# Two banks for scores, one pool of four banks for the other products, and a new written order in a decay-attention kernel with a gated convolution

## The chip, the core and the metric

The kernel runs on one core of a Trainium2 chip. The metric is device time in microseconds (us) of one execution; lower is better. A core has a matrix engine (TensorE, PE in the profile, with its weight loads as PEld), a vector engine (VectorE, DVE), an engine for functions (ScalarE, ACT), GpSimd (POOL) and SyncE (SP). In this kernel SP and POOL mostly issue transfers. Products of PE go to PSUM, which has eight banks of 128 x 512 float32. Only ACT and DVE take results out of it here.

## The reference, cut to what matters

Four batches, eight heads, 768 steps, head size 48. A state of 48 x 48 complex numbers decays step by step, takes in the outer product of key and value, and is read with the query. The result goes through a causal convolution of five taps, a sigmoid gate and two projections of 384 x 384. Everything is float32 and the weights of convolution and projections arrive as 64-bit numbers.

```python
mag = np.sqrt(a_re * a_re + a_im * a_im)
scale = np.minimum(mag, 0.999) / (mag + 1e-06)
a_re_n, a_im_n = (a_re * scale, a_im * scale)
for t in range(S):
    new_re = ar * S_re - ai * S_im
    new_im = ar * S_im + ai * S_re
    kv = np.einsum('bhd,bhe->bhde', k[:, :, t], v[:, :, t])
    S_re, S_im = (new_re + kv, new_im)
    y[:, :, t] = np.einsum('bhd,bhde->bhe', q[:, :, t], S_re)
...
for k in range(K):
    gate_pre += conv_w[k][None, None, :] * xp[:, k:k + S, :]
gate = 1.0 / (1.0 + np.exp(-gate_pre))
return (gate * (x @ w_val) @ w_out).astype(np.float32)
```

## The kernel before, in words

The decay of all steps up to t is a running sum of logarithms and angles, so the recurrence becomes a masked product of scaled queries and keys plus a carried state. The work is cut into ten units: eight groups of four heads, of which the first and the last are cut once more into two units of two heads. A unit goes through these steps, each named by a letter:

- **X, R, A, S, E, B** prepare it on ACT and DVE: logarithms, angles, sums along time (with small products on PE, `off`, that add the sums of earlier rows), sine and cosine, exponentials, and the scaled keys `kx` and queries (which take the place of `trig`). Small x, r, a are the same for odd units.
- **T** transposes one quarter of a head: three products with the identity into a tile `pt` (`L417`), which ACT copies into `kq` (`L418`). A unit of four heads has 16 of them, one of two heads 8.
- **s, k, t, y** work on a chunk of 128 steps, six to a unit: scores of keys and queries into `sc_ps` (`L445`, `L446`); the mask, by which DVE takes them out into `sm` (`L452`); the state, summed in `S_ps` and copied by ACT into `S_sb` (`L484` to `L487`); and the output in `y_ps`, from `sm` and the previous chunk's `S_sb`, copied by ACT into `y_sb` (`L465` to `L469`).
- **D** moves `y_sb` to the channel-major `xT` (`L499`, issued by POOL), **C** is the convolution on DVE (`L508`, `L511`), **G** the sigmoid on ACT, **M** one half of a projection step: the products `pv` with the first weight matrix, which DVE multiplies by the gate (`L532`), and `po` with the second, which ACT copies out (`L563`). **O** issues the store of the result.
- **W** converts the weights on DVE and ACT. **L, V, N** issue loads of inputs, values and re-laid keys, on SP.

The order in which all these steps are issued is the string `ORDER`, 991 letters long. Each letter asks its stream for one step; a step that may not go yet is passed over. At the end every instruction is tied to the one before it on its engine, so each engine works in the written order: an instruction that waits holds up all that stand behind it on that engine.

What binds the steps besides is the number of buffers. Scores have one bank (`PSC`), so the scores of a chunk may be issued only when the mask of the chunk before stands ahead of them, and run only when DVE has taken those out. The transposed tiles `pt` have two banks of their own. The pool `ps_m` has three, for `off`, `pv` and `po` (and `ps_t` lends a bank for `po` in the last batch). `S_ps` and `y_ps` have one each.

Of the kernel before, what the change touches and what calls it, by code (L numbers as in the profile page):

```python
# [22 lines left out]
    "XLXXLXxxxXXxxLxXxXRxrWLLWRRWLLRWWRAWRWrAWLWrAWrWRSSEErWaBWWrXWXWrSSWWXaWBBLWaXNWWWXVLNEWEWXBWWWW"  # L23
    "XTWXRRTRTTTRVWTtTWTBLRRtBskBWLLWRsWSWAStBxWLkTWAWyTxAskWyxWWTNETyskTETTytTtWBLtDBxxskysBLLtXksBT"
    "kxtWWXytTTyskNDxTTNWyXTTWXWskXxTtsVkyWXTDTXrytskTTWXRskrrRtytNTrTTtrTrRarSaskytLSDsRWaEVykRRERsk"
    "ytSsyBALBksBSLkBTCxsCyktTCDtNTxyTxTLTATxyTDTCxTLCtACTTtxTCTtTNCCTsCCCCCECxCkCVCGMMMMMsMyMksxrrrM"
    "EByMrLOMkstytBksrrBLXrDyMXkBLNMySMasTTkyTTDatXSTLOaCTNCCEMCTMTMXTMTXCMTTXtVTMTtTTEsBLtXCBOkMsBLX"
    "RyMkMxyxsBkRtTTyRtMxNRAsxxRTTkyAxstxtOkTxTNOrsTAkLTRDryMRSyLrMrTTaMTDOTtTTtTTsraaSECCCCCkCCCCCCC"
    "GMMMMMMsyEVkrMMsMOrSBLksyMOBNMMMByLMSkXysBXTkTtTTtEMTTyskTTyTTXXMtLXTTtNTTtTTsEBMDtLLDXCCBMksByM"
    "LxxkMyBskCtTXTsyVksxXCCRxtCTMORTNkDRyxMLtyRAsTTMxOkxRALyxrMTTAMtTrrMTRraTTtTTRtOTDCCCCCaCCOVrTrs"  # L30
    "kaCCCCCSSrSSGMMMMMMEsyEMkMsykMNyBDBsNBBTTktTOTsktCTtTCsTTCNMOykMECyMMCMCMysMksEBBBktMyMyOVstBkTT"
    "sMktNysktTTDCNCtCtyMytCMOTTsktTDCTsCkytDskyMsMkyMOyMDsMCCtMCCCCksCCCCCCGkOMstCyMCCCCCMGytkMMMyMM"
    "MMDOMOMMMMOCCCCCCGMMMMMMOMMOMOM"
# [12 lines left out]
def kernel(  # L46
# [33 lines left out]
    LB, MAINB, TMPB, KB, PSC, SMB, SSB, ZB, XB, KNB, VB, YB = 6, 3, 2, 6, 1, 2, 3, 4, 2, 3, 2, 2  # L80
    WL = 6
    TRIGB, KXB = 2, 1

# [7 lines left out]
    ps_t = fast.enter_context(tc.tile_pool(name="ps_t", bufs=2, space=PSUM))  # L91
    ps_s = fast.enter_context(tc.tile_pool(name="ps_s", bufs=PSC, space=PSUM))
    ps_S = fast.enter_context(tc.tile_pool(name="ps_S", bufs=1, space=PSUM))
    ps_y = fast.enter_context(tc.tile_pool(name="ps_y", bufs=1, space=PSUM))
    ps_m = fast.enter_context(tc.tile_pool(name="ps_m", bufs=3, space=PSUM))
# [132 lines left out]
    for t in y_ps + sc_ps:  # L228
        nc.vector.memset(t, 0.0)

# [172 lines left out]
    def transpose(u):  # L403

        b, h0, g = units[u]
        tl = tiles[u]
        for h in range(g):
            while not free_head():
                yield "wait"
            heads[0] += 1  # L410
            t = qkp.tile([C2, 2, S], F32, name="kq")
            tj = t.rearrange("c s (f p j) -> c s f p j", f=2, j=JH)
            for f in range(2):
                for s, src in enumerate((tl["kx"], tl["qx"])):
                    pt = ps_t.tile([P, JH, P], F32, name="pt")
                    for j in range(JH):
                        nc.tensor.transpose(pt[:C2, j, :], src[:, j, f, h, :], ident)  # L417
                    nc.scalar.copy(tj[:, s, f], pt[:C2].rearrange("c j p -> c p j"))  # L418
# [6 lines left out]
    class Attend:  # L425


        def __init__(self, u):
            self.u = u
            self.b, self.h0, self.g = units[u]  # L430
            self.tl = tiles[u]
            self.S_ps = None
            self.sc, self.sm, self.S_sb, self.y = {}, {}, {}, {}
# [40 lines left out]
        def state(self, n):  # L474
            if n == NCH - 1:
                return
            if n == 0:
                self.S_ps = ps_S.tile([P, 512], F32, name="S_ps")
            kn, vt = self.tl["kn"][n // HN], self.tl["v"]
            for h in range(self.g):  # L480
                c0 = (n % HN * self.g + h) * C2
                at_h = dict(start=(n == 0 and h == 0), stop=(n == NCH - 2), skip_group_check=True)
                cols = slice(h * D, (h + 1) * D)
                nc.tensor.matmul(self.S_ps[:64, cols], kn[:, c0:c0 + 64], vt[:, h, n], **at_h)  # L484
                nc.tensor.matmul(self.S_ps[64:C2 + 1, cols], kn[:, c0 + 64:c0 + C2 + 1], vt[:, h, n], **at_h)
            self.S_sb[n] = small.tile([C2, self.g * D], F32, name="S_sb", bufs=SSB)
            nc.scalar.copy(self.S_sb[n], self.S_ps[:C2, :self.g * D])  # L487
# [33 lines left out]
    def project(b, xT, t0, n, z, pool, psum, outs=None, ahead=None):  # L521
# [12 lines left out]
        if ahead:  # L534
            pvs = [psum.tile([P, 512], F32, name="pv", tag="mm") for _ in range(NT)]
# [19 lines left out]
        for m in range(t0, t0 + n, P):  # L555
            po = ps_t.tile([P, 512], F32, name="po", tag="pt") if ahead else psum.tile([P, 512], F32, name="po", tag="mm")
# [168 lines left out]
    def stream_c():  # L725
        for e in corder:
# [97 lines left out]
    def advance(key):  # L824
        if key in "skty":
# [160 lines left out]
```

## Time and profile before

| | us |
|---|---|
| median of three runs | 365.17 (364.27 to 367.84) |
| the profiled execution, its own time | 367.19 |
| span of its instructions | 365.5 |
| PE busy | 283.7 (78%) |
| DVE busy | 259.9 (71%) |
| ACT busy | 248.9 (68%) |
| POOL busy | 59.0 (16%) |

The durations used below are from the profiled execution, whose own time is 2.0 us over the median. PE stands still until the first unit is prepared (its first transposition starts at 31.4 us), and its last product ends at about 355 us; what remains of the span is the end of the program. A busy share is a mean over stretches with different limits, so the profile is read by stretches. The clock that PE was granted is either full or half; the profile gives its mean over a stretch.

### The profile page before, as it was taken

The numbers are of one execution on the slowest core, as the hardware profiler recorded it, in microseconds if no ns is written. First come the engines' busy times: TensorE is split into PE (matmuls) and PEld (weight loads), VectorE is DVE, ScalarE is ACT, GpSimd is POOL, SyncE is SP. The second block draws the span as 40 slices with busy tenths as digits, with TensorE's granted clock in tenths as the row PEclk, the third lists the DMA queues.
The fourth block names the chain that finished last, engine by engine and source line by source line (L and its number), as shares of the span: only waits on it lengthen the run. The fifth ranks groups of instructions, "written<-read, shape, count | busy, mean of one in ns | idle before, by whom it ended". The sixth has DMA issues, their size and how long they took to land.

```text
span 365.5 us, 8088 instructions
## 1 busy us (share of the span) xinstructions
PE 283.7 (78%) x3234; PEld 201.4 (55%) x3234; DVE 259.9 (71%) x339; ACT 248.9 (68%) x454; POOL 59.0 (16%) x147
## 2 busy tenths in 40 slices
PE   0120688486978699999979879999998999959970
PEld 0110466364766556756767447778765866745540
DVE  3699996837597799969886986389698657292310
ACT  5689678589599676998888777767978533441210
POOL 3000001011012200340123003302400340410210
PEclk9999996969799899999999989999999999988996
DMA  7944559778379752886949206669720526210210
GB/s 191 345 111 127 143 142 258 183 198 163 93 147 260 193 118 81 214 243 150 315 131 231 51 23 215 165 191 200 198 75 3 163 77 142 82 56 2 82 48 24
DMA packets 87804, 53.31 MB, mean 146 GB/s; under 512 B 36432, under 2 KB 84816, under 8 KB 87760
## 3 DMA queue, kind: packets, MB, share of 16 engines
q1 hardware_dynamic: 83664, 43.28, 45.8%
q0 software_dynamic: 4096, 9.44, 8.4%
q8 instruction: 27, 0.44, 0.5%
q14 instruction: 17, 0.14, 0.1%
HBM read 33.83 MB, written 14.16 MB: 131 GB/s over the span
## 4 chain that ended last, share of the span: by engine, by line
PE 23%; DVE 10%; issue 7%; DMA 6%; ACT 3%; POOL 2%; SPq 0%; POOLq 0%; DVEq 0%
PE po L242 6%; DVE z L511 4%; PE pt L417 3%; PE pv L242 3%; PE sc_ps L445 3%; DMA kn<-kd 3%; PE y_ps L465 3%; DMA xT<-y_sb 3%; PE y_ps L468 2%; POOL xT L499 1%; DVE kx L369 1%; DMA kd<-kx 1%; PE S_ps L484 1%; DVE z L508 1%; DVE sm L452 1%
## 5 line engine op out<-in xcount | busy, mean ns | idle before, releaser
L499 POOL DMA_DIRECT2D xT<-y_sb x80 | 40.6, 513 | 171.3 <-ACT y_sb L469 134.8
L418 ACT COPY kq<-pt 96x384 f32<-96x384 f32 x128 | 56.1, 476 | 17.6 <-PE pt L417 15.8
L452 DVE TENSOR_TENSOR sm<-sc_ps,mask 128x512 f32<-128x512 f32 (+1 forms) x60 | 34.8, 580 | 31.4 <-PE sc_ps L446 29.8
L242 PE MATMUL po<-wo_sb,z 128*64 128x384 f32 x288 | 52.1, 499 | 4.7 <-DVE z L532 4.6
L511 DVE SCALAR_TENSOR_TENSOR z<-xT,cw_sb,z 128x768 f32<-128x768 f32 (+1 forms) x60 | 51.4, 857 | 2.1
L445 PE MATMUL sc_ps<-kq 96*64 96x128 f32 x384 | 46.7, 287 | 7.9 <-DVE sm L452 7.8
L242 PE MATMUL pv<-xT,wv_sb 128*64 128x384 f32 x288 | 51.7, 505 | 0.0
L446 PE MATMUL sc_ps<-kq 96*64 96x64 f32 x384 | 44.5, 230 | 0.0
L417 PE MATMUL pt<-ident,kx 128*96 128x128 f32 x192 | 38.3, 314 | 8.0 <-DVE kx L369 7.6
L417 PE MATMUL pt<-ident,trig 128*96 128x128 f32 x192 | 36.2, 303 | 10.5 <-ACT tmp L284 5.4
L445 PEld LDWEIGHTS sc_ps<-kq 96*64 96x64 f32 x384 | 33.7, 143 | 18.0 <-DVE sm L452 12.5
L465 PE MATMUL y_ps<-kq,S_sb 96*48 96x128 f32 x320 | 36.7, 287 | 7.3 <-ACT y_sb L469 7.1
L468 PE MATMUL y_ps<-sm,v_in 128*48 128x128 f32 x384 | 41.2, 280 | 1.5 <-DVE sm L452 1.5
L469 ACT COPY y_sb<-y_ps 112x256 f32<-112x256 f32 (+1 forms) x60 | 19.5, 325 | 30.3 <-PE y_ps L468 28.9
L446 PEld LDWEIGHTS sc_ps<-kq 96*64 96x64 f32 x384 | 39.2, 142 | 0.0
L102 ACT ACT_TABLE_LOAD x28 | 35.9, 1283 | 1.3 <-PEq L970 0.8
L242 PEld LDWEIGHTS po<-wo_sb,z 128*64 128x64 f32 x288 | 24.0, 138 | 21.6 <-DVE z L532 6.6
L484 PE MATMUL S_ps<-v_in,kn 128*64 128x48 f32 x320 | 30.4, 234 | 6.1 <-ACT S_sb L487 4.2
L242 PEld LDWEIGHTS pv<-xT,wv_sb 128*64 128x64 f32 x288 | 22.6, 142 | 21.3 <-issue 14.6
L484 PEld LDWEIGHTS S_ps<-v_in,kn 128*64 128x64 f32 x320 | 25.4, 147 | 11.8 <-ACT S_sb L487 4.9
L417 PEld LDWEIGHTS pt<-ident,trig 128*96 128x96 f32 x192 | 23.1, 139 | 15.2 <-ACT kq L418 5.8
L417 PEld LDWEIGHTS pt<-ident,kx 128*96 128x96 f32 x192 | 21.2, 139 | 16.7 <-DVE kx L369 7.9
(83 smaller groups left out, 487.9 us busy)
## 6 DMA issues: line engine op xcount, KB each, us to landing
kd<-kx SPq DMA_DIRECT2D x12, 576.0 KB, 4.6
out_dram<-ot POOLq DMA_DIRECT2D x24, 192.0 KB, 2.4
ar_in<-in_a_re_dram SPq DMA_DIRECT2D x12, 288.0 KB, 4.0
ai_in<-in_a_im_dram SPq DMA_DIRECT2D x12, 288.0 KB, 5.9
k_in<-in_k_dram SPq DMA_DIRECT2D x12, 288.0 KB, 4.8
q_in<-in_q_dram SPq DMA_DIRECT2D x12, 288.0 KB, 4.5
xT<-y_sb POOLq DMA_DIRECT2D x48, 72.0 KB, 3.2
kd<-kx SPq DMA_DIRECT2D x8, 288.0 KB, 3.1
```

Source lines behind the costliest of these rows:

```text
L102: nc.scalar.preload_act_table_set(name)
L242: nc.tensor.matmul(out[c:c + 64], lhsT[:, c:c + 64], rhs, **kw)
L417: nc.tensor.transpose(pt[:C2, j, :], src[:, j, f, h, :], ident)
L418: nc.scalar.copy(tj[:, s, f], pt[:C2].rearrange("c j p -> c p j"))
L445: nc.tensor.matmul(sc[lo:lo + half, h, :], k[:, :half], q, start=True, stop=True)
L446: nc.tensor.matmul(sc[hi:hi + half, h, half:], k[:, half:], q[:, half:], start=True, stop=True)
L452: nc.vector.tensor_tensor(out=two(sm), in0=two(sc[:, :g]), in1=mask[:, :, None, :].to_broadcast([C, 2, g // 2, C]), op=ALU.mult)
L465: nc.tensor.matmul(o, self.S_sb[n - 1][:, h * D:(h + 1) * D], self.part(1, h, n), start=True, stop=False)
L468: nc.tensor.matmul(o, vt[:, h, n], sm[:, h, :], start=(n == 0), stop=True)
L484: nc.tensor.matmul(self.S_ps[:64, cols], kn[:, c0:c0 + 64], vt[:, h, n], **at_h)
L499: XQ.dma_start(out=xTs[b][c0 % P:c0 % P + c2 - c0, c0 // P, EXT + hf * HS:EXT + (hf + 1) * HS], in_=self.y[hf][r0:r0 + c2 - c0, h // 2],)
L511: nc.vector.scalar_tensor_tensor(out=z, in0=xT[:, c, EXT + t0 - t:EXT + t0 - t + n], scalar=cw_sb[:, TAPS - 1 - t, c:c + 1], in1=z, op0=AL ...
```

## The change

Five things are edited.

1. The scores get two banks (`PSC` 2): chunks take turns, and the scores of a chunk wait for the mask of the chunk before the last.
2. The pool `ps_t` of two banks is gone. `pt` now comes from `ps_m`, which has four banks instead of three. The sum of the banks is eight as before.
3. The state's bank is one tile for the whole kernel, `S_all`, set to zero once at the start by DVE, instead of a new tile for each unit.
4. `ORDER` is another string with the same letters, each as often as before (128 T, 104 M, 90 C, 60 each of s, k, t, y, and so on). Each kind of instruction on PE, DVE and ACT therefore comes as often as before, apart from one load of a function table more on ACT, and on DVE two more settings of a bank to zero. On POOL one small tile `zero` is set.
5. A function `keep_busy` is added, a product with zeros under the letter `w`. The letter does not stand in the new `ORDER`, so no such product is issued.

The core of the diff:

```diff
-    "XLXXLXxxxXXxxLxXxXRxrWLLWRRWLLRWWRAWRWrAWLWrAWrWRSSEErWaBWWrXWXWrSSWWXaWBBLWaXNWWWXVLNEWEWXBWWWW"
...
+    "LLXLXxxXXVxXLxxXXxxXRxrWWWWWLRWWRrrLWLVWRARRALWrarWraARSSWWWaWWWWWrSSEWEBBBLBWXWXEENXLNWTTTWTTWT"
...
-    LB, MAINB, TMPB, KB, PSC, SMB, SSB, ZB, XB, KNB, VB, YB = 6, 3, 2, 6, 1, 2, 3, 4, 2, 3, 2, 2
+    LB, MAINB, TMPB, KB, PSC, SMB, SSB, ZB, XB, KNB, VB, YB = 6, 3, 2, 6, 2, 2, 3, 4, 2, 3, 2, 2
+    MMB = 4
+    KEEP = 128
...
-    ps_t = fast.enter_context(tc.tile_pool(name="ps_t", bufs=2, space=PSUM))
-    ps_s = fast.enter_context(tc.tile_pool(name="ps_s", bufs=PSC, space=PSUM))
+    ps_t = None
+    ps_s = fast.enter_context(tc.tile_pool(name="ps_s", bufs=1, space=PSUM))
-    ps_m = fast.enter_context(tc.tile_pool(name="ps_m", bufs=3, space=PSUM))
+    ps_m = fast.enter_context(tc.tile_pool(name="ps_m", bufs=MMB, space=PSUM))
...
+    S_all = ps_S.tile([P, 512], F32, name="S_ps")
+    zero = const.tile([P, 64], F32, name="zero")
+    nc.gpsimd.memset(zero, 0.0)
-    for t in y_ps + sc_ps:
+    for t in y_ps + sc_ps + [S_all]:
         nc.vector.memset(t, 0.0)
+    def keep_busy():
+        nc.tensor.matmul(
+            S_all[:64, 512 - KEEP:], zero, dmat.rearrange("p f q -> p (f q)")[:, :KEEP],
+            start=False, stop=True, skip_group_check=True,
+        )
+        return True
...
-                    pt = ps_t.tile([P, JH, P], F32, name="pt")
+                    pt = ps_m.tile([P, 512], F32, name="pt", tag="mm")[:, :JH * P].rearrange("c (j p) -> c j p", j=JH)
...
-            if n == 0:
-                self.S_ps = ps_S.tile([P, 512], F32, name="S_ps")
...
-            po = ps_t.tile([P, 512], F32, name="po", tag="pt") if ahead else psum.tile([P, 512], F32, name="po", tag="mm")
+            po = psum.tile([P, 512], F32, name="po", tag="mm")
...
+        if key == "w":
+            return keep_busy()
```

How the new string moves instructions shows best at two places. The first is ACT where the copies of the sixth unit (unit 5 of 0 to 9) begin; `kq<-pt` is such a copy, `y_sb` and `S_sb` are the copies of an output and of a state, `ot` of a projection. Before:

```order
L469 COPY y_sb<-y_ps_133 112x2x128
L269 ACTIVATE tmp<-main 128x1152
L487 COPY S_sb<-S_ps 96x192
L418 COPY kq<-pt 96x384 x2
L469 COPY y_sb<-y_ps_133 112x2x128
L487 COPY S_sb<-S_ps 96x192
L563 COPY ot<-po 128x384
L276 ACTIVATE tmp,over<-main 128x1152
L279 ACTIVATE tmp<-tmp,b_one 128x1152
L418 COPY kq<-pt 96x384 x2
```

And now, at the same unit:

```order
L576 COPY ot<-po 128x384
L481 COPY y_sb<-y_ps_130 112x2x128
L292 ACTIVATE tmp<-tmp,b_one 128x1152
L431 COPY kq<-pt 96x384 x3
L481 COPY y_sb<-y_ps_130 112x2x128
L497 COPY S_sb<-S_ps 96x192
L431 COPY kq<-pt 96x384 x13
```

The 16 copies of a unit came in pairs between other steps and now come almost in one run, and their transpositions with them on PE. Outputs, states and projections that stood among the copies stand ahead of them or behind.

The second place is PE near the end of the last unit, from the scores of its fourth chunk on. `sc_ps_134` is the one bank of scores before; `sc_ps_131` and `sc_ps_132` are the two of now. Each row with `L445` or `L446` (now `L457`, `L458`) is a product of scores, and a chunk of this unit has four. Before:

```order
L485 MATMUL S_ps<-v_in,kn 33x48
L445 MATMUL sc_ps_134<-kq 64x128
L446 MATMUL sc_ps_134<-kq 64x64
L445 MATMUL sc_ps_134<-kq 64x128
L446 MATMUL sc_ps_134<-kq 64x64
L445 MATMUL sc_ps_134<-kq 64x128
L446 MATMUL sc_ps_134<-kq 64x64
L445 MATMUL sc_ps_134<-kq 64x128
L446 MATMUL sc_ps_134<-kq 64x64
L484 MATMUL S_ps<-v_in,kn 64x48
```

Now, where the last chunk's scores stand:

```order
L494 MATMUL S_ps<-v_in,kn 64x48
L495 MATMUL S_ps<-v_in,kn 33x48
L255 MATMUL pv<-xT,wv_sb 64x384 x12
L457 MATMUL sc_ps_132<-kq 64x128
L458 MATMUL sc_ps_132<-kq 64x64
L457 MATMUL sc_ps_132<-kq 64x128
L458 MATMUL sc_ps_132<-kq 64x64
L494 MATMUL S_ps<-v_in,kn 64x48
```

Before, the scores of two chunks stood back to back on one bank, so that the second had to wait for the mask of the first. Now twelve products `pv` and the chunk before stand between a bank's scores and its next ones.

More of the change, by code (lines that the diff above doesn't have):

```diff
@@ L22 @@
 ORDER = (
-    "XLXXLXxxxXXxxLxXxXRxrWLLWRRWLLRWWRAWRWrAWLWrAWrWRSSEErWaBWWrXWXWrSSWWXaWBBLWaXNWWWXVLNEWEWXBWWWW"
[L24 to L33, printed above, removed]
+    "LLXLXxxXXVxXLxxXXxxXRxrWWWWWLRWWRrrLWLVWRARRALWrarWraARSSWWWaWWWWWrSSEWEBBBLBWXWXEENXLNWTTTWTTWT"
+    "XTXTBLsskBXBWkyLWtBTskNXXLtRRxRyWskWWsWxTTxTRykWtRTxWxWxTWWTyLsWkWRtWTxytskxrrDyAttWsksARNSyktSr"
+    "DVysWtrAErysWrkWDErBLatBskSatBLyLSkaNByXEWWXyNWTTtDTTTTTTLTWTTTTXTTTtEstBLXsVBktkyXWsBLkWyBskxtX"
+    "yDstykWskNXytxWCCCCCTTXTyTTDTTTTxCCTCTTTTVTCTsktCxskCCLCCtNyCxCskCRRCLGMRMMsxtMykMxMyDRAARRsxrrr"
+    "ktRSSMMAOMMstrEEOryMrMBLMMrSSBNyaMBLLLOaXMtkXMMaMyMEMDBTTTTTTTTTTTTXTTXTTstEBLMsNtBkykBLxsOMxsNt"
+    "yVksXBkXtCysxkXtXyMxMkyxTTTyttTOCTTTTTCTTCTCMDDCOTNxTCTCTCCCCLRCCRCskRstCxCCGMMMMMMRskRtVykLRxrr"
+    "rMMORsykAMSyrDMSAAEaOrskrtMrMsOaEBMtLBNykMSyMaMtSEBLLXyBNXMMTTMTTTTTTLTTTTTTTTsEtMXDBLsXBkkBLXLx"
+    "txXyskCtysBXMOtCXRRyDskRxkCNtTtTVTTTTTTsxxRAyLRxCkCMANxRxrrAyMMMMOyDtTVTTTTTrTTRSSssCCktCyskCras"
+    "kECtOyCCsEBkrBCCtCCyDBskCtykNCGMaMaMMyMtByMCCCMMOCCCtTDTTTTTTTMsksrtrCNCSMVMCSskMMykOMCMMEEBCOsB"
+    "NsBtNMykMMCykMDyMstBTTTTTOTTkTtstykMyDssMtykkMMOtMCCyCsCksCtCCCCCCCOykDCtCCMGCCMstyMMCGMMyMkyMMt"
+    "MDMOOMMMMMOCCCCCCGMMMMMMMMOOMMO"
 )
@@ L431, in __init__ @@
             self.tl = tiles[u]
-            self.S_ps = None
             self.sc, self.sm, self.S_sb, self.y = {}, {}, {}, {}
@@ L483, in state @@
                 cols = slice(h * D, (h + 1) * D)
-                nc.tensor.matmul(self.S_ps[:64, cols], kn[:, c0:c0 + 64], vt[:, h, n], **at_h)
-                nc.tensor.matmul(self.S_ps[64:C2 + 1, cols], kn[:, c0 + 64:c0 + C2 + 1], vt[:, h, n], **at_h)
+                nc.tensor.matmul(S_all[:64, cols], kn[:, c0:c0 + 64], vt[:, h, n], **at_h)
+                nc.tensor.matmul(S_all[64:C2 + 1, cols], kn[:, c0 + 64:c0 + C2 + 1], vt[:, h, n], **at_h)
             self.S_sb[n] = small.tile([C2, self.g * D], F32, name="S_sb", bufs=SSB)
-            nc.scalar.copy(self.S_sb[n], self.S_ps[:C2, :self.g * D])
+            nc.scalar.copy(self.S_sb[n], S_all[:C2, :self.g * D])
         def collect(self, hf):
@@ L534, in project @@
         if ahead:
-            pvs = [psum.tile([P, 512], F32, name="pv", tag="mm") for _ in range(NT)]
+            pvs = [
+                psum.tile([P, 512], F32, name="pv", tag="mm")
+                for i in range(NT)
+            ]
             for ci in range(NT):
@@ L733, in stream_c @@
                 zs[b, c] = moe.tile([P, S], F32, name="z", bufs=ZB)
+                done["z", b, c] = True
             yield from conv(xTs[b], t0, n, c, zs[b, c][:, t0:t0 + n])
@@ L752, in stream_m @@
             if i in early:
-                while not (has_x(b, 0, t0 + n) and done.get("W") and done.get(("T", NU - 1)) and (b, NT - 1) in zs):
+                while not (has_x(b, 0, t0 + n) and done.get("W") and done.get(("T", NU - 1)) and done.get(("z", b, NT - 1))):
                     yield "wait"
```

## The prediction

> **What bounds the kernel now.** I read the page first, for the busy tenths of its 40 slices (9.1 us each) and the granted clock.
>
> ```profile
> PE   0120688486978699999979879999998999959970
> ACT  5689678589599676998888777767978533441210
> PEclk9999996969799899999999989999999999988996
> ```
>
> PE is nearly full in the second half and not in the first; ACT is the other way round. So I looked for the point where one takes over from the other, and found it at the copies of unit 5's transpositions. The next two fences are the timeline of ACT there and the stretches to either side (stretch: length, then busy time and count of PE, PEld, DVE, ACT and POOL, the granted clock, DMA).
>
> ```profile
> 179.42 0.30 ACT L487 COPY S_sb<-S_ps 96x192 f32<-96x192 f32 x1
> 179.62 0.86 ACT L418 COPY kq<-pt 96x384 f32<-96x384 f32 x2
> ```
>
> ```profile
> 31.40:179.60 148.20, 117.39 (x1326) 84.91 (x1328) 121.78 (x140) 119.72 (x206) 18.62 (x44) 0.92 0.70 180
> 179.60:355.00 175.40, 163.20 (x1880) 113.89 (x1877) 116.20 (x160) 106.00 (x216) 36.48 (x80) 0.97 0.43 116
> ```
>
> The copy at 179.62 follows the instruction before it with no idle time: ACT was the late one. Up to there each of the three engines is busy for 117 to 122 of 148 us, and none is full: a chain through all three sets the pace. From there PE is busy for 163.2 of 175.4 us, ACT and DVE for 106 and 116. The end is thus the moment at which ACT comes to unit 5's copies, plus what PE has left by then, plus some 12 us in which PE still stands idle.
>
> **The change part by part.** I make the sum against this execution, in differences, and apply them to the median: the execution took 367.19 us, 1.7 more than its span of 365.5, and 2.0 more than the median of 365.17.
>
> *What PE has left at unit 5.* In the written order of the two kernels I counted what stands on each engine ahead of unit 5's first transposition. On PE it is now, beyond what stood there before, six products `po` (one step), the scores and the outputs of three chunks of four heads, and the state of one. The timeline of a full stretch gives their prices by the starts.
>
> ```profile
> 244.90 2.11 PE L242 MATMUL po<-wo_sb,z 128*64 128x384 f32 x12
> 246.84 0.42 PE L465 MATMUL y_ps<-kq,S_sb 96*48 96x128 f32 x4
> 247.72 0.27 PE L445 MATMUL sc_ps<-kq 96*64 96x128 f32 x1
> 248.39 0.27 PE L484 MATMUL S_ps<-v_in,kn 128*64 128x48 f32 x2
> 248.93 0.53 PE L417 MATMUL pt<-ident,kx 128*96 128x128 f32 x3
> ```
>
> So `po` is 1.94, an output 0.88, scores 0.67, a state 0.54, and the sum is 1.94 + 3 x 0.88 + 3 x 0.67 + 0.54 = 7.1 us that PE no longer has ahead of it when unit 5 begins. On ACT the same count gives three `y_sb`, two `ot`, one `S_sb` and one full-width activation more, and two table loads less.
>
> ```profile
> L102 ACT ACT_TABLE_LOAD x28 | 35.9, 1283 | 1.3 <-PEq L970 0.8
> L469 ACT COPY y_sb<-y_ps 112x256 f32<-112x256 f32 (+1 forms) x60 | 19.5, 325 | 30.3 <-PE y_ps L468 28.9
> L563 ACT COPY ot<-po 128x384 f32<-128x384 f32 x24 | 11.5, 480 | 17.9 <-PE po L242 16.6 <-issue 1.2
> L511 DVE SCALAR_TENSOR_TENSOR z<-xT,cw_sb,z 128x768 f32<-128x768 f32 (+1 forms) x60 | 51.4, 857 | 2.1
> L487 ACT COPY S_sb<-S_ps 96x192 f32<-96x192 f32 (+1 forms) x50 | 14.2, 284 | 12.0 <-PE S_ps L485 8.1 <-PE S_ps L484 2.4
> L279 ACT ACTIVATE tmp<-tmp,b_one 128x1152 f32<-128x1152 f32 (+1 forms) x10 | 10.6, 1064 | 0.2
> ```
>
> That is 3 x 0.33 + 2 x 0.48 + 0.28 + 1.06 - 2 x 1.28 = +0.7 us on ACT (the groups' means, with `L279` for the activation). On DVE four `L511`, one `L508` and one full-width step less stand ahead of unit 5's keys: at 0.86 each 5.2 us, an estimate by the `L511` row. If ACT reaches that point as before, 0.7 us later, the end comes 7.1 - 0.7 = **6.4 us** earlier. Bounds: nothing, if PE itself holds back the first stretch, where it now does 7.1 us more (it has 148.2 - 117.4 = 30.8 us idle there to take them in); 12 us, if DVE's 5 us are the ones that count (7.1 + 5). I take 6.4, as ACT was the late engine.
>
> *Two score banks.* These are PE's waits from 190 us on, and the place of the longest.
>
> ```profile
> PE po L242 <- DVE z L532: 4.6, 2, 3.5
> PE sc_ps L445 <- DVE sm L452: 4.1, 3, 2.7
> ```
>
> ```profile
> 322.72 0.32 PE L445 MATMUL sc_ps<-kq 96*64 96x128 f32 x1 [1.22 <-DVE sm L452]
> 326.00 0.48 PE L445 MATMUL sc_ps<-kq 96*64 96x128 f32 x1 [2.72 <-DVE sm L452]
> 327.95 6.23 PE L242 MATMUL pv<-xT,wv_sb 128*64 128x384 f32 x24
> 333.99 0.42 PE L465 MATMUL y_ps<-kq,S_sb 96*48 96x128 f32 x4
> ```
>
> Scores wait 1.22 and 2.72 us for the mask, which on DVE stands behind a convolution. The 24 `pv` behind them take 6.04 us from start to start, where 2 x 1.94 would do: they run at half clock, 2.2 us lost. In the new order a bank's next scores stand behind 12 `pv`, an output, two states and other scores, over 5 us of PE, while the mask needs one `L508`, three half-width `L511` and itself, under 3 us. So this wait goes, 1.22 + 2.72 + 2.2 = **6.1 us**, in a stretch that PE bounds. What is late next is the mask for the output `y_ps`; its output stands behind another `po` or `pv` (1.94 us) and should be covered; if it is not, up to all 6.1 comes back. Bounds 0 and 6.1, and I take 6.1, the only place that the trace shows.
>
> *One pool for four kinds of tile.* Four transposed tiles in a row now share banks with `off`, `pv` and `po`. PE waits in order, so when a bank is still held everything behind it stops. Before, with two banks, transpositions waited for copies as follows; a copy's price is in the second row, two tiles' on PE in the third.
>
> ```profile
> PE pt L417 <- ACT kq L418: 5.1, 5, 2.3
> L418 ACT COPY kq<-pt 96x384 f32<-96x384 f32 x128 | 56.1, 476 | 17.6 <-PE pt L417 15.8
> ```
>
> ```profile
> 287.10 0.79 PE pt L417 x6
> ```
>
> Two bounds: four banks instead of two could take away a part of the 5.1, say -2; or the shared banks add as much again, +5. In the order every `off` and nearly every `pv` that a transposition follows in its bank is released on DVE ahead of the keys and queries that the transposition needs anyway. That leaves little: I take **+1**.
>
> *Transpositions in runs.* A run of 16 copies costs ACT 56.1 / 128 = 0.44 us each. PE does two tiles in 0.79 us, 0.40 each (last row, from the chain of waits), so PE idles 16 x 0.04 = 0.6 us a run with nothing else to do. Five runs from unit 5 on, two of them half as long, make 2.4 us at most; before, part of it was paid too. **+1**. What the clock does in a run is a rival, below.
>
> *At no cost.* Two settings of a bank more are 0.97 us on DVE at the start; DVE idles 1.42 us there, before its first product.
>
> ```profile
> 3.46 0.48 DVE L229 MEMSET sc_ps<- 128x512 f32 x1
> 5.36 0.76 DVE L271 TENSOR_TENSOR main<-tmp,ai_in 128x576 f32<-128x576 f32 x1 [1.42 <-ACT tmp L269]
> ```
>
> Were that cover gone, they would cost the 0.97. `zero` is one small setting on POOL that nothing waits for. One tile for the state asks for the same copies ahead of the same products. Loads go through SP in an order of their own, and stand as far ahead of their use as before where I counted (from a unit's key product to the second next unit's first logarithm, some 7 us of engine work in both). `keep_busy` is never called.
>
> The sum: -6.4 - 6.1 + 1 + 1 = -10.5, and 365.2 - 10.5 = 354.7, **355 us**.
>
> **The rivals.**
>
> *The clock falls in the runs of transpositions (slower).* The clock was halved after stretches in which PE did little. The next fence has a stretch with little work and what came after it, one with many transpositions and what came after that, and the half clock near the end; the fence behind it has the first and the third row's stretch with the instructions on `pt` alone.
>
> ```profile
> 86.60:89.90 3.30, 1.18 (x17) 0.78 (x16) 2.52 (x3) 3.29 (x7) 0.00 (x0) 1.00 1.30 207
> 90.00:100.00 10.00, 8.43 (x100) 6.43 (x100) 6.17 (x8) 5.49 (x11) 0.00 (x0) 0.66 0.48 111
> 113.80:117.20 3.40, 2.57 (x29) 1.88 (x27) 2.67 (x4) 3.40 (x9) 0.00 (x0) 1.00 1.08 276
> 117.20:120.60 3.40, 2.67 (x28) 1.95 (x28) 1.75 (x3) 1.45 (x4) 0.00 (x0) 1.00 0.23 60
> 325.40:332.20 6.80, 6.20 (x38) 3.84 (x40) 3.68 (x8) 1.55 (x4) 0.00 (x0) 0.51 0.00 0
> ```
>
> ```profile
> 86.60:89.90 3.30, 0.04 (x1) 0.00 (x0) 0.76 (x2) 1.00 1.30 207
> 113.80:117.20 3.40, 1.52 (x13) 1.01 (x11) 1.50 (x4) 1.00 1.08 276
> ```
>
> After 1.18 us of work in 3.3 the clock fell (0.66 in the next 10 us); after 2.57 in 3.4, of which 1.52 were transpositions, it held at 1.00. If transpositions didn't count as work, the latter would have had 2.57 - 1.52 = 1.05, less than the former, and the clock should have fallen. That speaks against the rival. But no stretch of before is nothing but transpositions, and a run of 16 is 6.4 us. Price: after the fall near the end half clock lasted 6.8 us (0.51, last row), which loses 3.4. Six units of four heads would lose 20 us: 355 + 20 = 375. It decides from five runs on, 17 us: 372 is over 1% slower. The Trainium skill has this as a rule (TensorE: Matmul & The Clock Gate, Part 4: PE-mode transpose): full clock doesn't engage for transposes, which don't count as busy the same way. By that rule this case would be the forecast; by the two rows it is not, and I give it 8 in 100.
>
> *The waits only move (no change).* ACT may reach unit 5 as much later as PE has more to do before, and the masks come as late for the outputs as they came for the scores. Then 6.4 and 6.1 go, +2 stays or not: 365 to 367. For it speaks that the three engines are evenly loaded up to 179.6 us, so that no order has much room. 18 in 100.
>
> *The first stretch gets shorter too (faster still).* These are PE's longest waits from 60 to 190 us.
>
> ```profile
> PE y_ps L465 <- ACT y_sb L469: 4.3, 3, 2.0
> PE S_ps L484 <- ACT S_sb L487: 4.2, 1, 4.2
> PE pt L417 <- ACT kq L418: 3.4, 4, 2.3
> PE sc_ps L445 <- DVE sm L452: 3.1, 6, 0.8
> ```
>
> They are 15 us, and half clock follows several of them. The forecast counts none of it. With the scores looser (3.1) and chunks further apart, a half of these, 7 to 8 us, may go and be passed on to ACT: 347. Likewise the 4.6 us for `z` after 190. 17 in 100.
>
> **How the numbers follow.** Of 100, the forecast has 50, faster still 17, no change 18, the fallen clock 8, and 7 remain for places of the new order that I have not found, mostly to the slow side. About 1%, 3.7 us, is what a measurement of this kernel can tell from no change, so the borders are 361.5 and 368.8. The forecast's own range is 349 (12 instead of 6.4 for unit 5) to 362 (the second term lost, the first kept, with the +1 of the pool): 47 of its 50 are faster, 3 within. Faster still gives 17; no change 3, 14 and 1; the fallen clock, with two or three runs only, 1 within and 7 slower; the rest 2 within and 5 slower. In all 0.67 faster, 0.20 within 1%, 0.13 slower. The range for 8 in 10 goes from 341, below which some 4 of the faster case's 17 lie (all 15 us of those waits gone), to 368, the upper end of no change with 1 us: above it are the fallen clock's 7, the rest's 5 and 1 of no change. That leaves out 17.
>
> **What the profile after would show.** Unit 5's first copy stands at about 180 us, with some 7 us less of PE behind it; if it stands at 187, the first step was wrong. PE's waits of scores for masks are under 1 us after 190, and none of the waits of `y_ps` for masks has taken their place; the `pv` near the end run at 1.94 a dozen. Transpositions behind `off` or `pv` don't wait for DVE. In the runs of copies the granted clock stays full, and the slices after them too. The prediction is wrong as a whole if PE is not the full engine from unit 5 on.

## The result and the profile after

The changed kernel takes 353.76 us (median of 4 runs, 351.17 to 356.22) where the kernel before took 366.50 in the same series (4 runs): a ratio of 0.9645, with a 95% interval from 0.9539 to 0.9752. It is faster, by 12.7 us; the forecast was 355. Medians are over all runs of a kernel, and ratios leave out slow runs, those over 1.5% above the kernel's fastest. The profiled execution is the shortest of the four: it took 351.17 us, 1.8 more than its span of 349.4.

The first fence is the page of the changed kernel: the busy tenths of PE and ACT and the granted clock, in 40 slices of 8.7 us. The second is ACT's timeline at unit 5's first copy, the third the stretches to either side of it, with the columns of the prediction's fence (length, then busy time and count of PE, PEld, DVE, ACT and POOL, the granted clock, DMA).

```profile
PE   0033757668977999996669999979989999999960
ACT  5758789999657899987357989956996457553110
PEclk9999887956989999999968999996999999999995
```

```profile
178.56 1.26 ACT L292 ACTIVATE tmp<-tmp,b_one 128x1152 f32<-128x1152 f32 x1
179.71 1.22 ACT L431 COPY kq<-pt 96x384 f32<-96x384 f32 x3
```

```profile
31.40:179.60 148.20, 115.97 (x1444) 95.38 (x1445) 120.77 (x140) 120.03 (x213) 21.44 (x49) 0.89 0.71 186
179.60:339.00 159.40, 149.90 (x1757) 112.38 (x1755) 113.46 (x159) 104.29 (x211) 34.65 (x75) 0.97 0.47 120
```

The copy stands at 179.71 where it stood at 179.62, so between these two executions the whole gain lies behind it. There PE is busy for 13.3 us less (163.20 to 149.90) and idle for 2.7 less (12.2 to 9.5). Of the 13.3, the prediction's count of moved work is 7.1; the other 6.2 are equal products in less time, 2.0 of them the `pv`, some of which ran at half clock before. A second profiled execution of the changed kernel, of 354.05 us, bears out the stretch behind the copy (156.8 us to PE's last product, where this one has 157.7 and the kernel before 174.8), but has the copy at 183.4. The time of the copy thus changes by some 4 us from one execution to the next, and the median of 353.76 lies nearer to that second execution.

These are PE's waits from 190 us on, and the group of the transpositions' copies.

```profile
PE y_ps L480 <- DVE sm L464: 3.4, 3, 2.1
PE sc_ps L457 <- DVE sm L464: 0.3, 1, 0.3
```

```profile
L431 ACT COPY kq<-pt 96x384 f32<-96x384 f32 x128 | 51.8, 508 | 4.4 <-PE pt L430 4.2
```

Scores wait 0.3 us for masks where they waited 4.1. Outputs now wait 3.4 for the same masks, and the 4.6 us of `po` behind `z` are gone. ACT's idle time ahead of copies fell from 17.6 to 4.4 us.

What I had not expected stands on DVE. Its timeline at the first use of the loads of `ai` for units 6, 7 and 8 comes first, then the output on PE that waits for the mask at 175.56, then what stood on SP's queue.

```profile
154.62 1.36 DVE L284 TENSOR_TENSOR main<-tmp,ai_in 128x1152 f32<-128x1152 f32 x1 [6.34 <-DMA ai_in<-in_a_im_dram]
...
174.28 1.36 DVE L284 TENSOR_TENSOR main<-tmp,ai_in 128x1152 f32<-128x1152 f32 x1 [6.02 <-DMA ai_in<-in_a_im_dram]
175.56 0.69 DVE L464 TENSOR_TENSOR sm<-sc_ps,mask 128x512 f32<-128x512 f32 x1
...
229.42 0.76 DVE L284 TENSOR_TENSOR main<-tmp,ai_in 128x576 f32<-128x576 f32 x1 [5.87 <-DMA ai_in<-in_a_im_dram]
```

```profile
176.30 0.45 PE L480 MATMUL y_ps<-sm,v_in 128*48 128x128 f32 x1 [4.88 <-DVE sm L464]
```

```profile
144.24 4.33 SPq L413 DMA_DIRECT2D kn<-kd  x3
148.63 1.22 SPq L114 DMA_DIRECT2D ai_in<-in_a_im_dram  x2
...
155.77 8.05 SPq L413 DMA_DIRECT2D kn<-kd  x3
163.92 1.23 SPq L392 DMA_DIRECT2D kd<-kx  x2
165.20 2.72 SPq L114 DMA_DIRECT2D ai_in<-in_a_im_dram  x2
```

Over the whole run DVE waits 21.4 us in five places for `ai_in`; before it was 3.6 in three. The `ai` loads stand behind groups of `kn` loads that keep SP for 4 to 8 us. These waits became one of the two questions of the experiments. The other was whether the two terms of the sum, order and score banks, are what I took them for.

### The profile page after: what moved, and what is told of

The parts are those of the page before. It is cut to its first block, busy times and chain, and to the rows that moved or that the text cites. A ratio compares the mean times of both kernels' runs of the same rounds, so it can differ in the third digit from the quotient of the medians.

```text
span 349.4 us, 8122 instructions
## 1 busy us (share of the span) xinstructions
PE 269.5 (77%) x3234; PEld 210.8 (60%) x3234; DVE 257.9 (74%) x341; ACT 245.7 (70%) x455; POOL 60.1 (17%) x148
## 4 chain that ended last, share of the span: by engine, by line
DMA 24%; DVE 19%; PE 18%; ACT 16%; issue 9%; SPq 8%; POOL 2%; POOLq 0%; DVEq 0%; ACTq 0%
DMA kn<-kd 14%; SPq L114 4%; ACT L104 4%; PE pt L430 3%; PE pv L255 3%; PE po L255 3%; ACT kq L431 3%; DVE sm L464 3%; DVE z L521 2%; DMA kd<-kx 2%; DVE kx L382 2%; DVE main L379 2%; DMA raw<-in_moe_w_val_dram 2%; SPq L413 2%; PE sc_ps L457 2%
## 5 line engine op out<-in xcount | busy, mean ns | idle before, releaser
L431 ACT COPY kq<-pt 96x384 f32<-96x384 f32 x128 | 51.8, 508 | 4.4 <-PE pt L430 4.2
L480 PE MATMUL y_ps<-sm,v_in 128*48 128x128 f32 x384 | 44.0, 294 | 10.2 <-DVE sm L464 10.2
L255 PE MATMUL pv<-xT,wv_sb 128*64 128x384 f32 x288 | 49.8, 486 | 0.0
L457 PE MATMUL sc_ps<-kq 96*64 96x128 f32 x384 | 43.2, 286 | 1.7 <-DVE sm L464 1.7
L477 PE MATMUL y_ps<-kq,S_sb 96*48 96x128 f32 x320 | 38.5, 300 | 7.3 <-ACT y_sb L481 5.1
L458 PE MATMUL sc_ps<-kq 96*64 96x64 f32 x384 | 43.3, 229 | 0.0
L458 PEld LDWEIGHTS sc_ps<-kq 96*64 96x64 f32 x384 | 40.1, 143 | 2.0
L457 PEld LDWEIGHTS sc_ps<-kq 96*64 96x64 f32 x384 | 33.6, 145 | 4.6 <-DVE sm L464 2.1
L255 PEld LDWEIGHTS pv<-xT,wv_sb 128*64 128x64 f32 x288 | 25.8, 137 | 16.1
L480 PEld LDWEIGHTS y_ps<-sm,v_in 128*48 128x48 f32 x384 | 28.6, 133 | 11.2 <-DVE sm L464 11.2
L430 PEld LDWEIGHTS pt<-ident,kx 128*96 128x96 f32 x192 | 24.1, 144 | 14.4 <-issue 11.9
L477 PEld LDWEIGHTS y_ps<-kq,S_sb 96*48 96x48 f32 x320 | 22.6, 132 | 15.6 <-ACT y_sb L481 8.1
```

The source lines that it names most:

```text
L255: nc.tensor.matmul(out[c:c + 64], lhsT[:, c:c + 64], rhs, **kw)
L457: nc.tensor.matmul(sc[lo:lo + half, h, :], k[:, :half], q, start=True, stop=True)
L458: nc.tensor.matmul(sc[hi:hi + half, h, half:], k[:, half:], q[:, half:], start=True, stop=True)
L477: nc.tensor.matmul(o, self.S_sb[n - 1][:, h * D:(h + 1) * D], self.part(1, h, n), start=True, stop=False)
L480: nc.tensor.matmul(o, vt[:, h, n], sm[:, h, :], start=(n == 0), stop=True)
```

## The experiments

The ratio is always to the kernel before in the same series (medians there 364.74, 363.5, 363.86 and 363.99). The last three columns cut the profiled execution into the time of unit 5's first copy, from there to the end of PE's last product, and from there to the end of the span; they are empty for three kernels whose profiled execution lies some 3 to 7 us over the median.

| kernel | median, us | ratio, 95% interval | copy at | PE behind it | closing |
|---|---|---|---|---|---|
| before | 366.5 | 1 | 179.6 | 174.8 | 11.1 |
| changed | 353.8 | 0.9645 (0.9539 to 0.9752) | 179.7 | 157.7 | 11.9 |
| changed, again | 351.3 | 0.9658 (0.9586 to 0.9731) | | | |
| old order, new banks | 360.8 | 0.9879 (0.9837 to 0.9922) | 181.7 | 167.4 | 11.6 |
| new order, old banks | 396.0 | 1.0837 (1.0786 to 1.0889) | 191.3 | 192.2 | 11.1 |
| changed, one score bank | 388.4 | 1.0601 (1.0535 to 1.0667) | 190.5 | 184.3 | 12.3 |
| all angle loads on POOL | 349.4 | 0.9571 (0.9518 to 0.9624) | 182.0 | 156.2 | 8.4 |
| the same from unit 3 on | 345.1 | 0.9492 (0.9401 to 0.9583) | 178.1 | 153.4 | 8.1 |
| the same, `v` of unit 5 earlier | 342.9 | 0.9393 (0.9335 to 0.9451) | | | |
| `kn` behind `ai` on SP | 350.9 | 0.9665 (0.9585 to 0.9744) | 180.6 | 154.8 | 12.2 |
| 27 fillers in PE's waits | 355.5 | 0.9820 (0.9749 to 0.9892) | 178.5 | 159.7 | 12.4 |
| 18 of them, first place | 352.5 | 0.9713 (0.9658 to 0.9767) | 180.7 | 155.4 | 12.1 |
| three `po` into unit 5 | 365.6 | 1.0041 (0.9996 to 1.0085) | | | |
| 32 fillers where PE is full | 355.7 | 0.9740 (0.9663 to 0.9816) | 181.8 | 160.0 | 12.4 |

### Order and banks apart

The old order with the new banks:

```diff
--- the changed kernel
+ORDER = (the 991 letters of the kernel before)
```

> The order of before, with the banks of the changed kernel (two for scores, one pool of four for pt, off, pv and po). Theory of the prediction: the second bank takes away the waits of scores for masks near the end (1.22 and 2.72 us) and the 2.2 us of half clock behind them, and the pool of four costs or gains 1 to 2: some 6 us less than before, 359 to 361, with under 2 us left of the 7.8 us that scores waited for masks in the whole run. Rival, that two banks are of use only in an order written for them: the waits pass to the outputs y_ps, which need the same masks one step later; 364 to 367, within 2 us of before.

The new order with the old banks, in which a chunk's scores that stood ahead of the mask before them follow it:

```diff
--- the changed kernel
-    MMB = 4
+    MMB = 3
-    ps_t = None
+    ps_t = fast.enter_context(tc.tile_pool(name="ps_t", bufs=2, space=PSUM))
-    sc_ps = [... for i in range(PSC)]
+    sc_ps = [... for i in range(1)]
-            self.sc[n] = sc = sc_ps[(self.u * NCH + n) % PSC]
+            self.sc[n] = sc = sc_ps[0]
-                    pt = ps_m.tile([P, 512], F32, name="pt", tag="mm")...
+                    pt = ps_t.tile([P, JH, P], F32, name="pt")
+            po = ps_t.tile(..., tag="pt") if ahead else psum.tile(..., tag="mm")
-        if key in "skty":
+        if key in "sk":
+            late[0] += key == "s"
+            got = key == "s" or chunk("k")
+            while late[0] and at["s"] == at["k"]:
+                late[0] -= 1
+                chunk("s")
+            return got
+        if key in "ty":
```

> The new order with the banks of before: one bank for scores, two for pt, three for the rest. The order of PE differs from the changed kernel's at three places only, where the scores of a chunk stand ahead of the mask of the chunk before; they stand right behind it here. Theory of the prediction: the order alone is worth its first term, 6.4 us, and the waits of scores for masks are there as in before (some 8 us in all, 6 of them where PE sets the end): 358 to 361. Rival, that the order does nearly all of it: within 2 us of the changed kernel, 352 to 356.

And the changed kernel with one score bank, its pool of four kept (of the diff above only `range(1)`, `sc_ps[0]` and the last nine lines):

> The changed kernel with one bank for scores (at the same three places the scores stand behind the mask) and its pool of four banks left as it is. It parts the score bank from the pool. Theory of the prediction, in which the pool costs 1 us and the second bank gains 6: some 359 to 361, and 1 us over the kernel with the new order and all banks of before. Rival, that the pool of four is what the new order needs: within 2 us of the changed kernel, 352 to 356, and the kernel with the old banks 4 us or more behind it.

The first gave 360.84, inside the forecast of 359 to 361. The other two gave 395.96 and 388.43, some 30 us beyond either theory. The first two fences show the stretch behind unit 5's copy and PE's one wait of scores in the old order with new banks. The other two are PE's waits in the new order with old banks, and in the changed kernel with one score bank.

```profile
181.70:350.20 168.50, 158.95 (x1867) 112.14 (x1864) 115.57 (x159) 105.64 (x216) 36.34 (x80) 0.99 0.43 118
```

```profile
PE sc_ps L457 <- DVE sm L464: 0.9, 1, 0.9
```

```profile
PE sc_ps L457 <- DVE sm L464: 41.4, 24, 7.5
...
PE pt L430 <- ACT kq L431: 13.9, 41, 1.8
```

```profile
PE sc_ps L457 <- DVE sm L464: 49.6, 24, 9.8
...
PE pt L430 <- ACT kq L431: 0.6, 1, 0.6
```

So the two parts don't add. With two banks the new order is worth 9.7 us behind the copy (167.4 to 157.7). With the old banks it costs 31 us, as the chunks' scores wait 24 times for masks that the new order lets come late. In the traces PE's order with one bank differs from the changed kernel's in the scores of four chunks (the expectations say three places): two of unit 4, one each of units 8 and 9. What the second bank buys at all the other places is that a product may run ahead of a mask that DVE has not reached yet. The old order waits 7.8 us without it, the new one 41.4. The pool of four gives 7.5 us between the last two kernels: the 13.9 us in 41 waits of transpositions for copies fall to 0.6.

### The loads of the angles

All loads of `ar` and `ai` from unit 2 on, by POOL's queue:

```diff
         for f in range(2):
-            nc.sync.dma_start(
+            issuer.dma_start(
+        # with, ahead of the loop:
+        issuer = XQ if nm in ("ar", "ai") and u > 1 else nc.sync
```

> The changed kernel, with the loads of ar and ai from unit 2 on issued on POOL's queue instead of SP's, where they stand behind kn loads that wait for kd. In the changed kernel DVE stands 2.3, 0.9, 6.3, 6.0 and 5.9 us waiting for ai_in, and PE 4.9 and 2.1 us for masks behind two of these waits, with half clock after both. Theory: SP's order is the cause; the waits of 6 us fall to 3 or less, and the time by 4 to 9 us, to 345 to 350. Rival, that what limits is the transfers' own rate (other transfers move at the same time): the landings take as long, the waits stay over 4 us each, and the time stays at 352 to 356, or rises, where loads on POOL stand behind transfers that wait there.

It gave 349.43, between the two. DVE's waits for `ai_in` of the units from 2 on are gone. But the start is later. The fence is DVE's first instruction on the weights, in the changed kernel and then, in a fence of its own, in this one.

```profile
13.98 0.36 DVE L186 TENSOR_SCALAR cvt<-raw 128x384 uint32<-128x384 uint32 x1 [0.66 <-DMA raw<-in_moe_w_val_dram]
```

```profile
18.97 0.36 DVE L187 TENSOR_SCALAR cvt<-raw 128x384 uint32<-128x384 uint32 x1 [5.35 <-DMA raw<-in_moe_w_val_dram]
```

Unit 2's angles, which nobody needs before 28 us, went out at 6.6 us beside the weights and held them up by 5.0. Next, unit 2's stay on SP (`u > 2` in the diff), in one series with the changed kernel unaltered:

> The changed kernel with the loads of ar and ai on POOL's queue from unit 3 on (unit 2's stay on SP's). With unit 2's there too, they went out at 6.6 and 9.3 us, and DVE waited 5.35 us for w_val at 18.97 us, where it has 0.66 at 13.98; all units up to 4 then ran 5 to 9 us late. Theory: DVE's waits for ai_in are gone as there and the start is as in the changed kernel, so unit 5's first copy comes at 172 to 178 us and the time is 340 to 346. Rival: the first stretch has other limits by then (the three engines' own work, kn loads), the copy stays at 179 to 182, and the time at 346 to 351.

> The changed kernel itself, unaltered, as the measure for the other kernels of this series. 350 to 356 by every theory.

The start is 1.6 us late instead of 5.0 (that first instruction stands at 15.57), and the time is 345.07 against 351.26, a gain of 6.2. Unit 5's copy came at 178.1, at the very edge of what I expected. In the third series I moved one letter more: `v` of unit 5 goes ahead of the first of three groups of `kn` loads on SP's queue (the `V` at place 481 of the order stands at 462).

> The changed kernel with ar and ai on POOL's queue from unit 3 on and one letter moved: the v loads of unit 5 stand on SP's queue ahead of three groups of kn loads instead of behind two of them. With the first alone PE waited 3.0 and 1.6 us for v_in at 179 to 184 us, and the clock was halved from 183.4 to 186.8. Theory: both go, 3 to 6 us less than with the first alone, 338 to 342 where that gave 345. Rival: the state's other operand, kn, comes last instead, since it stands behind the v loads: no gain, 343 to 347.

342.9 us, 0.9393 of the kernel before: the lowest median here. In its profiled execution, of 349.66 us and so 6.8 over the median, no wait for `v_in` is left on PE; waits for `kn` stand in their place, the rival's mechanism. Its gain on the kernel without the letter (0.9492) is within the two intervals and not shown.

Are the waits for `ai_in` what the 6.2 us come from? For that, the order alone was changed, no queue: three letters `N` behind the next `ar` or `ai` load.

```diff
 # places of the letters in the order of the changed kernel
-N at 414, 464 and 614
+N behind the L at 419, 471 and 627
```

> The changed kernel with three letters of the order moved: the kn loads of unit 4 (both halves) and the first of unit 6 stand behind the next ar or ai loads on SP's queue instead of ahead of them. No queue is changed. Theory, that ai_in is late because it stands behind kn loads which wait for kd and for each other: DVE's waits of 6.3, 6.0 and 5.9 us fall by 2 to 5 each, the kn loads come as much later, and the time is 2 to 6 us below the changed kernel. Rival, that the transfers share the same rate: the waits for ai_in shrink and waits of the state S_ps for kn take their place, within 2 us of the changed kernel or above it.

DVE's waits for `ai_in` fell from 21.4 to 3.4 us, as the theory has it, and the time stayed at 350.93. The waits of PE from 150 to 250 us say why:

```profile
PE S_ps L494 <- DMA kn<-kd: 3.5, 1, 3.5
PE S_ps L495 <- DMA kn<-kd: 2.7, 1, 2.7
PE off L255 <- DVE main L249: 2.6, 2, 2.3
PE S_ps L494 <- ACT S_sb L497: 2.3, 1, 2.3
```

That is 11.1 us in the place of the 8.6 that outputs waited for masks there, and 6.2 of it are the state's waits for `kn`, which were 0.5 in the changed kernel. The rival's outcome came, though by these runs not for its reason: on POOL's queue the `ai` loads took no less time to land (a median of 6.0 us, 5.2 on SP's), and the waits went all the same. What makes them wait is their place on SP's queue, and on one queue `kn` comes later where `ai` comes earlier. And of the gain of the loads on POOL from unit 3 on, the larger part is not a wait at all. The table has 3.8 us of it in the closing stretch, behind PE's last product. The rows are those of the program's last line, in the changed kernel and then in the kernel with the loads on POOL from unit 3 on (durations in ns, least, median, longest).

```profile
L997 POOLq DRAIN  x3: 40/107/8559, 340.0 to 349.1; - x3
```

```profile
L998 POOLq DRAIN  x3: 46/107/4474, 334.4 to 339.4; - x3
```

POOL closes with 8.56 us in the one and 4.47 in the other: 4.1 of the 6.2. What the waits for `ai_in` cost on the path is thus about 2 us by the medians, not the 4 to 9 of my theory. The two ratios leave some 4 us of room to either side of that (an estimate from their intervals), so it may also be nothing.

### What half clock costs

In the changed kernel PE works 1.2 to 1.5 of 3.41 us ahead of each fall of the clock but the last, which comes behind its last product. In every trace here the changes of the clock lie whole multiples of 3.41 us apart, such as 6.83 and 10.24, so work is counted in stretches of that length. The function `keep_busy`, which the change adds and never calls, fills such waits with products with zeros; nothing is added to the result.

```diff
 # letters of the order
+18 x w ahead of the 29th y (the output that waits at 171 to 176 us)
+ 9 x w ahead of the 37th y (the output that waits at 232.6 to 234.7 us)
```

> The changed kernel with 27 calls of keep_busy, 18 ahead of the output that waits at 171 to 176 us and 9 ahead of the one that waits at 232.6 to 234.7 us: products with zeros that add nothing to the result and fill PE's wait. Theory: half clock follows a stretch of 3.4 us with PE busy for 1.5 or less; with the waits filled the clock stays full at 173.6 to 180.5 and 235.1 to 241.9, and the second, where PE sets the end, gives back some 2 to 3 us: 350 to 352. Rival: the products behind the wait are held by masks and copies of DVE and ACT anyway, so full clock there only makes PE wait: within 1 us of the changed kernel. If the clock falls in spite of the filled waits, the reading of the clock is wrong.

It came out slower than the changed kernel, 355.46. The trace shows a mishap at the second place: the products write the state's tile, and wait there for ACT's copy of it, which stands behind a load of `ar`.

```profile
235.58 0.69 PE L238 MATMUL S_ps<-dmat,zero 128*64 128x128 f32 x2 [5.42 <-ACT S_sb L497]
```

So the first place alone:

> The changed kernel with 18 calls of keep_busy (products with zeros, nothing added to the result) ahead of the output that waits at 171 to 176 us, and none at the second place of the run before, where they waited 5.4 us for a copy of the state. Theory: the clock stays full from 173 to 187 us, unit 6's first copy comes some 3 us earlier than in the changed kernel, as in the run before (220.3 against 223.1), and the end 2 to 3 us: 348 to 350. Rival: what is won at full clock is lost again before the end, at the half clock after 235 us, where DVE's wait for ai_in sets the time: 350 to 354.

The fences show the stretch around it in this kernel, then in the changed one.

```profile
168.20:175.00 6.80, 6.80 (x120) 5.90 (x117) 2.87 (x4) 3.83 (x7) 2.88 (x5) 1.00 0.90 253
175.00:181.80 6.80, 6.64 (x79) 6.04 (x77) 6.69 (x8) 4.20 (x9) 0.00 (x0) 1.00 0.76 134
```

```profile
166.70:173.60 6.90, 4.72 (x74) 3.55 (x69) 1.56 (x2) 2.25 (x5) 2.51 (x5) 1.00 1.02 284
173.60:180.50 6.90, 4.20 (x26) 3.38 (x28) 6.15 (x7) 3.83 (x8) 0.00 (x0) 0.51 0.54 106
```

The clock stayed full, so it was read rightly, and unit 6's first copy came at 221.0 instead of 223.1. PE's last product ends at 336.0 where it ended at 337.4, so in this execution 1.4 of the 2.1 us reached the end. The median, 352.5 with a ratio of 0.9713 against 0.9658, shows no gain. A gain of 1 or 2 us would be lost in that, so the rival, that what is won there is lost before the end, is neither shown nor refuted; the 2 to 3 us of the theory did not come.

### Is PE the bound behind unit 5?

Three products `po` and their copies moved back from ahead of unit 5's transpositions into them:

```diff
 # letters of the order
-M at 434, 436, 462, 475, 498 and 500, O at 474 and 511
+MMMOMMOM behind the T at 520
```

> The changed kernel with three products po (18 matmuls, 3 x 1.94 = 5.8 us of PE) and their three copies ot (3 x 0.48 = 1.4 us of ACT) moved from ahead of unit 5's transpositions into them. It does the reverse of the prediction's first step. Theory of that step (the end is the moment at which ACT comes to unit 5's copies, plus what PE has left): the copy comes up to 1.4 earlier and the end 4.4 to 5.8 later, some 355 to 357 against 351 for the changed kernel in the series before. Rival: PE takes the products into its 8 us of idle time after 180 us, or they fill waits for copies within the run of transpositions: 350 to 353.

365.59 us, 14 more than the changed kernel, where the theory had 4.4 to 5.8. The reason is another: the two letters `O` that I moved along put two writes of the output on POOL ahead of the transfers of `y_sb` into `xT`. In the profiled execution (368.58 us, 3.0 over the median) unit 5's copy comes at 183.4, as in the changed kernel's second one, and these transfers go out at 194.88 where they went out at 186.58 there. First DVE, then POOL:

```profile
202.36 0.62 DVE L518 TENSOR_SCALAR z<-xT,cw_sb 128x768 f32<-128x768 f32 x1 [15.15 <-DMA xT<-y_sb]
```

```profile
192.41 0.56 POOL L813 DMA_DIRECT2D out_dram<-ot  x1 [36.52 <-ACT ot L576]
194.35 0.55 POOL L813 DMA_DIRECT2D out_dram<-ot  x1 [1.37 <-ACT ot L576]
194.88 3.50 POOL L509 DMA_DIRECT2D xT<-y_sb  x7
```

DVE's convolution stood for 15.15 us. The run tells nothing on the first step; it shows what a transfer that is moved with a step does to the queue that it joins. So the question was put with work that no other engine has to do with: four calls of `keep_busy` ahead of each of eight states of units 7 and 8.

```diff
 # letters of the order, ahead of the t of the chunks 42, 43, 45, 46, 49, 50, 52 and 53
+wwww
```

> The changed kernel with 32 calls of keep_busy (products with zeros, nothing added to the result; 0.227 us each in the run before, 7.3 us in all), four ahead of each of eight steps of the states of units 7 and 8, between about 250 and 310 us, where PE is full. The reverse of the prediction's first step, with work that no other engine has to do with. Theory: PE's work behind unit 5's first copy sets the end, so all 7.3 us come back, less what falls into a wait: 356 to 359 where the changed kernel had 351 in its last series. Rival: the masks, copies and transfers there have as little room as PE, and their waits take the products in: 351 to 354.

The fence has the stretch from unit 7's first copy to PE's end, in this kernel, and then in the changed one.

```profile
244.20:341.70 97.50, 96.47 (x1093) 70.67 (x1091) 60.71 (x104) 51.45 (x117) 23.42 (x51) 1.00 0.35 89
```

```profile
245.00:337.40 92.40, 90.00 (x1029) 63.43 (x1027) 60.72 (x104) 51.33 (x117) 23.31 (x51) 1.00 0.37 94
```

Of 7.3 us, 5.1 came back at the end (97.5 against 92.4; 4.2 against the 93.3 of the changed kernel's second execution), and 3 to 4 in the medians (0.9740 against 0.9658 of the kernel before; 355.69 us against 351.26 in another series). The intervals of the two ratios overlap, so the medians alone don't show it. By the traces it is the theory's side, though at the median just below its range: from unit 7 on the larger part of the added work comes back at the end, and a third or so is taken in by waits. Between the copies of units 5 and 7, where PE is busy for 59.8 of 65.3 us, nothing of the kind was measured.

## Why the prediction was right

**What bounds the kernel** was read rightly: PE is nearly full behind unit 5's first copy, and of work given to it from unit 7 on the larger part comes back at the end.

**First step, PE's work ahead of unit 5 (-6.4).** Right in place, and the count holds: the copy came as before in one execution and 3.8 us later in the other, and the order was worth 9.7 us behind it with the new banks, against 7.1 counted. Not all of the 9.7 is the counted work: the 4.6 us of `po` behind `z` went too, which the third rival had, and 3.4 of outputs behind masks came. What the step left unsaid is that it holds only with the second bank. Taken as a term of its own, as the sum had it, it fell: alone the order costs 31 us.

**Second step, two score banks (-6.1).** The mechanism was right, the size too large. In the old order the new banks, the pool of four among them, bring 7.4 us behind the copy, of which 3.2 are scores' waits (4.1 to 0.9) and 2.2 the `pv`, and the clock there rises from 0.97 to 0.99. In that execution the copy came 2.1 later, and the medians have 3.9 in all, 364.74 to 360.84 (by the interval 2.8 to 5.9), where the sum had 6.1 - 1 = 5.1 for bank and pool. No run parts the two in the old order. That the outputs' waits would not take their place was half right: in the changed kernel they took 3.4 us, of which 2.1 stand behind the `ai` load at 229.42, and none where the scores had waited.

**The shared pool (+1).** The sign was wrong as far as the runs show it. Transpositions wait 0.3 us for copies in the changed kernel's whole run where they waited 5.1, which is more than my lower end of -2 could hold; in the new order with one score bank the pool gives 7.5 us. With two score banks no run measures it alone. Behind 180 us transpositions wait for DVE once, 0.7 us for `trig`, as forecast. I had weighed what might hold a bank and not that four banks let PE run four tiles ahead of ACT. **The runs of transpositions (+1)** can't be told apart from it: ACT's idle time ahead of copies fell by 13 us.

**At no cost.** Here a step failed: "Loads go through SP in an order of their own, and stand as far ahead of their use as before". By the engine work that I counted they do; but SP's queue has groups of `kn` loads between, and DVE's waits for the loads grew from 3.6 to 21.4 us. DVE's 5 us, which the first term's outer bound of 12 had counted on, may have gone there; no run shows that. On the path the waits cost about 2 us by the medians, or nothing.

**The rivals.** *The clock falls in the runs of transpositions* is refuted as a cause. The first fence is the changed kernel's stretches (columns as before), the second the first of them with the instructions on `pt` alone.

```profile
149.80:153.20 3.40, 3.40 (x30) 2.54 (x27) 0.00 (x0) 3.40 (x11) 1.25 (x5) 1.00 1.12 267
153.20:156.60 3.40, 3.40 (x51) 2.61 (x50) 1.98 (x2) 1.75 (x5) 0.00 (x0) 1.00 1.10 306
170.20:173.60 3.40, 1.22 (x10) 0.48 (x6) 0.00 (x0) 0.00 (x0) 0.31 (x1) 1.00 1.04 288
173.60:177.00 3.40, 0.70 (x8) 0.69 (x10) 2.72 (x3) 1.32 (x3) 0.00 (x0) 0.51 0.04 11
```

```profile
149.80:153.20 3.40, 3.40 (x30) 2.54 (x27) 3.40 (x11) 1.00 1.12 267
```

A stretch of nothing but transpositions leaves the clock at 1.00; one with 1.22 us of work halves it. The rule of the Trainium skill (TensorE: Matmul & The Clock Gate, Part 4: PE-mode transpose), by which transposes don't engage the full clock, is not borne out by this trace. The Trainium skill says it there of the engine's transpose mode; the trace calls these products MATMUL and doesn't show whether they ran in that mode. The forecast's sign that the clock stays full in every run of copies did fail once: in unit 5's run it was half from 183.9 to 187.3 us, behind a stretch in which PE waited for `v_in` and worked 1.38 of 3.40 us.

```profile
180.50:183.90 3.40, 1.38 (x25) 1.06 (x22) 2.93 (x3) 0.80 (x3) 1.73 (x4) 1.00 0.67 145
183.90:187.30 3.40, 3.40 (x22) 3.18 (x23) 2.41 (x3) 1.75 (x5) 1.77 (x4) 0.50 0.64 174
```

*The waits only move* did happen between scores and outputs (in the whole run 7.8 to 1.7 us for the ones, 1.5 to 10.2 for the others), but most of the new ones lie ahead of unit 5, where PE has room. *The first stretch gets shorter too* did not: 148.2 us hold the same work of DVE and ACT as before.

The sum came out 2 us short of the result, and that is in part luck. Bank and pool were taken for 5.1 us and gave 3.9; the order and its runs of transpositions were taken for 5.4 and gave some 8.5 with the new banks (an estimate from the ratios 0.9879 and 0.9645). The two errors go against each other, and the terms add only in that sequence, banks first: the order first would have cost 31 us. In the first profiled execution the differences were larger than in the median (-17.1 behind the copy, +0.9 in the closing, where the last copy waits for its buffer); the median's interval is 9.1 to 16.9 us.

## What to carry to other kernels

Don't add the worth of an order and of the buffers that it was written for: here the order alone cost 31 us, the buffers alone gave a third of the whole, and both together gave the 12.7. When an order moves, read each queue's own sequence for what stands *between* two transfers and how long that holds the queue; the distance in engine work doesn't show it. And a wait that goes is worth only what the next one on the same queue or bank leaves of it: three letters took 18 us of DVE's waits away and none from the end that the medians show.

## What the runs showed of the hardware

Transpositions count as work for the clock. I cut the 14 profiled executions into stretches of 3.41 us, starting from a change of the clock. In 51 of them PE did nothing but transpositions (over 3.0 us of them, under 0.3 of anything else); full clock followed on every one, also on the 15 that began at half clock.

The clock needs no idle stretch to fall. It fell after stretches with up to 1.97 us of work in 3.41 and never held with less than 1.45; between the two both were seen. To come back it took a stretch with at least 2.8 us, and it was seen to stay half after one with 3.16.

POOL's closing DRAIN (the longest of the three in the rows of `L997` and `L998`) took 8.56 us in all 11 kernels' executions with 104 transfers on POOL's queue, the kernel before among them, 5.45 in the one with 136 and 4.47 in the two with 132. It lies behind everything else, so it is 2% of the time that no engine's work explains. What sets it was not tried and stays open.
